# Hashing the later two pairs of a batch with GpSimd products and VectorE sums

## The chip, the cores and the metric

The kernel runs on one core of a Trainium2 chip. The metric is the device time of one execution in microseconds. The core has five engines that work side by side, each through its own queue in program order: TensorE (PE, with its weight loads as PEld), VectorE (DVE), ScalarE (ACT), GpSimd (POOL) and SyncE (SP), which here only issues DMAs. An engine whose next instruction waits does nothing else meanwhile.

## The reference, cut to what matters

Attention over 4 batches, 8 heads, 768 tokens and 64 dimensions, in which a query sees only the keys of its own hash bucket, followed by a gated feed-forward network with a residual:

```python
q_bits = (np.einsum('bhsd,dk->bhsk', q, proj) > 0).astype(np.int64)   # proj: 64 x 6
k_bits = (np.einsum('bhsd,dk->bhsk', k, proj) > 0).astype(np.int64)
...
mask = q_bucket[:, :, :, None] == k_bucket[:, :, None, :]
scores = np.where(mask, scale * q @ k.T, -1e9)
attn = exp(scores - max) / (sum + 1e-9);  x = attn @ v
g = x @ w_gate; val = x @ w_val
ffn_out = (gelu(g) * val) @ w_out
out = x + sigmoid(x @ w_res) * ffn_out
```

The hash gives six sign bits to each token and head: each is the sign of a product of a token's 64 numbers with a column of proj. It is computed in fp32.

## The kernel before, in words

Heads are handled in pairs, four pairs (p) to a batch, sixteen in all. "Side" 0 is q and side 1 is k. For one (pair, side) a tile `ld` of 128 partitions x 12 chunks x 64 holds the two heads' tokens. It is prepared in this way:

- `cast` (POOL, L184 for q and L186 for k) writes it as bf16 into the first 64 columns of a chunk of a `nat` tile. There are four `nat` tiles for all pairs, so that the later two pairs of a batch write where the earlier two were.
- `tr` (VectorE, L194) transposes 32 x 32 blocks of it into a `t32` tile, so that the 64 dimensions of 32 tokens stand on partitions, in two halves.
- `hash_mm` (TensorE, L205) multiplies `t32` with `projw`, a copy of proj in four blocks. One product of four (pair, side) jobs sits side by side; a call of `hashed` makes 16 of them, 32 matmul records.
- `hash_tok` (VectorE, L215) transposes the sums back, and `bits` (L224), four small instructions, one for each 32 partitions, writes +0.5 or -0.5 behind the 64 columns in `nat`.
- `turn` (L248) transposes `nat` into `aug` by a DMA that SP issues. `aug` is the operand of the score products, in which the bits make up the mask.

Each of the four batches goes through two stages. In the *scores stage* there are 36 slots, nine for a pair. A slot has the score products (`scores`, L380), an exponential on ScalarE (L385), some products of the previous batch's output projection (`project`: L431, L445, with VectorE's L448 and L451 after each of six token tiles), and the products with v of two slots ago (`values`, L354). After a head's values VectorE divides (`finish`, L306 and L307). A head's output buffer begins with a memset on VectorE (`opened`, L321), a product on TensorE (`preset`, L329) two slots later, and a copy on VectorE (`repeat`, L333), which the head's first values wait for. In slots counted from a stage's start, the memsets stand at 3, 7, 12, 16, 21, the copies at 5, 9, 14, 18, 23, and the first three L448 at 6, 13 to 14 and 21. Pair 2's scores begin at slot 18 and pair 3's at slot 27. ScalarE is busy for some 92% of this stage.

In the *gate stage* (`gate_val`) there are twelve steps m: eight products with w_gate and as many with w_val (L399), a Gelu on ScalarE (L416) and a product `hh` on VectorE (L419), which frees the buffer that the next step's w_val products need.

The order of everything else is written out by hand in two tables. `at(s, ...)` puts pieces behind the values of slot s, and `gv(b, m, ...)` puts them behind `hh` of step m of batch b's gate stage. For batch b + 1 the tables call its first two pairs `xs` and its later two `ys`. The x side is transposed and cast in the last slots of batch b's scores stage, hashed at the stage's end and in step 0, and gets its bits and turns in steps 0, 1, 2 and 4. The y side is transposed in slots 32 and 34 and in steps 3 and 5, cast in steps 5 and 6, hashed in step 6 (`hashed`), and gets its bits and turns in steps 7 to 10. The sums and the casts of v (`vals_s`: L281 to L285, `vals_a`: L273 and L274, all POOL) stand at slot 9p - 8. Weights are loaded by DMAs that POOL issues (L169); the last six stand in batch 0's gate stage, in steps 0, 0, 4, 5, 6 and 7. The first batch's own hash is done in another way and with TensorE, and does not change.

## Time and profile before

| | us |
|---|---|
| three runs | 346.91, 347.18, 347.49 (median 347.18) |
| span of the profiled execution | 344.9 |
| TensorE busy | 334.2 (97%) |
| ScalarE busy | 206.7 (60%) |
| VectorE busy | 191.4 (56%) |
| GpSimd busy | 86.3 (25%) |
| batch 0: scores stage, gate stage | to 47, 47 to 82.4 |
| batch 1: scores stage, gate stage | 82.4 to 125, 125 to 162.4 |
| batch 2: scores stage, gate stage | 162.4 to 205, 205 to 242.1 |
| batch 3: scores stage, gate stage and output | 242.1 to 285, 285 to 344.9 |

The page lists the profiled execution by its span alone, from its first to its last instruction; the times of the runs also hold what lies around it. In a line of the time line the first number is the start and the second the time from the start of the first to the end of the last instruction of the group; in square brackets stands how long the engine was idle before it, and whom it waited for. In a line of the groups stand the total, the mean of one in ns, and the idle time ahead with its releasers.

### The profile page before, as it was taken

The numbers are of one execution on the slowest core, as the hardware profiler recorded it, in microseconds if no ns is written. First come the engines' busy times: TensorE is split into PE (matmuls) and PEld (weight loads), VectorE is DVE, ScalarE is ACT, GpSimd is POOL, SyncE is SP. The second block draws the span as 40 slices with busy tenths as digits, with TensorE's granted clock in tenths as the row PEclk, the third lists the DMA queues.
The fourth block names the chain that finished last, engine by engine and source line by source line (L and its number), as shares of the span: only waits on it lengthen the run. The fifth ranks groups of instructions, "written<-read, shape, count | busy, mean of one in ns | idle before, by whom it ended". The sixth has DMA issues, their size and how long they took to land.

```text
span 344.9 us, 7549 instructions
## 1 busy us (share of the span) xinstructions
PE 334.2 (97%) x3064; PEld 204.3 (59%) x3112; DVE 191.4 (56%) x403; ACT 206.7 (60%) x232; POOL 86.3 (25%) x162
## 2 busy tenths in 40 slices
PE   7999999999999999999999999999999999999994
PEld 5667665655666655655666665655566665656442
DVE  7877757755345856757344784747244444333333
ACT  3789973226999962224999982323999984223110
POOL 4779940371055000270044100242030000000000
PEclk9999999999999999999999999999999999999999
DMA  7979999999375833528366642626330220000022
GB/s 224 376 62 219 205 276 217 197 139 193 103 188 172 204 106 78 102 38 149 82 193 188 231 115 65 128 48 113 72 100 32 55 55 30 32 1 0 32 77 76
DMA packets 71171, 42.90 MB, mean 124 GB/s; under 512 B 49504, under 2 KB 68192, under 8 KB 71136
## 3 DMA queue, kind: packets, MB, share of 16 engines
q1 hardware_dynamic: 64720, 37.17, 42.9%
q0 software_dynamic: 6336, 5.24, 10.8%
q8 instruction: 24, 0.39, 0.4%
q14 instruction: 11, 0.09, 0.1%
q10 hardware_dynamic: 80, 0.00, 0.0%
HBM read 29.36 MB, written 6.29 MB: 103 GB/s over the span
## 4 chain that ended last, share of the span: by engine, by line
PE 88%; ACT 4%; DVE 2%; DMA 2%; issue 2%; SPq 1%; POOL 0%; DVEq 0%; ACTq 0%
PE sp L399 36%; PE fps L445 18%; PE sp L380 15%; PE av L354 8%; PE rps L431 6%; ACT e L385 4%; PE hs L205 3%; DMA ld<-in_k_dram 2%; PE pt L259 1%; DVE o L451 1%; DVE nat L224 0%; SPq L96 0%; DVE o L448 0%; DVE ht L215 0%; DVE hh L419 0%
## 5 line engine op out<-in xcount | busy, mean ns | idle before, releaser
L385 ACT ACTIVATE e<-sp 128x1024 bf16<-128x1024 f32 x144 | 143.6, 1027 | 13.5 <-PE sp L380 8.0
L416 ACT ACTIVATE gt<-sp 128x768 bf16<-128x768 f32 x48 | 38.9, 811 | 92.5 <-PE sp L399 92.5
L380 PE MATMUL sp<-aug,aug 71*128 71x256 bf16 (+1 forms) x384 | 86.1, 325 | 1.1 <-ACT e L385 0.6
L445 PE MATMUL fps<-wo,hh 128*128 128x512 bf16 (+2 forms) x274 | 74.7, 369 | 1.6
L419 DVE TENSOR_TENSOR hh<-gt,sp 128x768 bf16<-128x768 bf16 x48 | 45.8, 954 | 50.1 <-PE sp L399 46.1
L399 PE MATMUL sp<-x_sb,wv 128*128 128x512 bf16 (+1 forms) x379 | 70.6, 325 | 0.4 <-DVE hh L419 0.2
L399 PE MATMUL sp<-x_sb,wg 128*128 128x256 bf16 (+1 forms) x373 | 70.4, 324 | 0.7
L354 PEld LDWEIGHTS <-e 128*128 128x128 bf16 x1152 | 53.3, 97 | 28.9 <-issue 1.2
L354 PE MATMUL av<-va,e 128*128 128x65 bf16 x1152 | 58.7, 193 | 0.1
L399 PEld LDWEIGHTS <-wv 128*128 128x128 bf16 x384 | 37.6, 98 | 25.1 <-issue 0.3
L399 PEld LDWEIGHTS <-wg 128*128 128x128 bf16 x384 | 36.8, 98 | 26.2 <-issue 2.3
L445 PEld LDWEIGHTS <-hh 128*128 128x128 bf16 x300 | 27.4, 97 | 22.7 <-issue 0.2
L448 DVE SCALAR_TENSOR_TENSOR o<-th,fps 128x512 f32<-128x512 f32 (+2 forms) x25 | 16.6, 666 | 36.6 <-PE fps L445 31.0
L380 PEld LDWEIGHTS <-aug 71*128 71x128 bf16 x384 | 29.4, 97 | 10.9 <-issue 2.2
L184 POOL TENSOR_SCALAR nat<-ld 128x768 bf16<-128x768 f32 (+1 forms) x16 | 13.8, 861 | 78.0 <-DMA aug<-nat 74.6
L281 POOL TENSOR_TENSOR v<-ldv 128x384 f32<-128x384 f32 x16 | 16.0, 999 | 67.7 <-DMA ldv<-in_v_dram 67.6
L194 DVE STREAM_TRANSPOSE t<-ld 128x768 f32<-128x768 f32 (+1 forms) x34 | 31.0, 916 | 1.4 <-DMA ld<-in_q_dram 0.7
L333 DVE COPY av<-av 128x390 f32<-128x390 f32 x24 | 13.6, 567 | 29.8 <-PE av L329 29.8
L431 PE MATMUL rps<-wr,x_sb 128*128 128x512 bf16 x90 | 25.3, 378 | 0.2
L435 ACT ACTIVATE th<-rps 128x512 f32<-128x512 f32 x24 | 14.2, 594 | 18.4 <-PE rps L431 18.4
L224 DVE TENSOR_SCALAR nat<-htp 32x72 bf16<-32x72 f32 x96 | 21.9, 229 | 1.8
L307 DVE TENSOR_TENSOR x_tok<-av,rec 128x384 bf16<-128x384 f32 x32 | 17.8, 557 | 1.1
(61 smaller groups left out, 190.7 us busy)
## 6 DMA issues: line engine op xcount, KB each, us to landing
ldv<-in_v_dram SPq DMA_DIRECT2D x16, 384.0 KB, 5.4
out_dram<-o SPq DMA_DIRECT2D x23, 256.0 KB, 2.0
ld<-in_q_dram SPq DMA_DIRECT2D x15, 384.0 KB, 5.4
ld<-in_k_dram SPq DMA_DIRECT2D x15, 384.0 KB, 6.2
wg<-in_moe_w_gate_dram POOLq DMA_DIRECT2D x4, 384.0 KB, 10.2
wv<-in_moe_w_val_dram POOLq DMA_DIRECT2D x4, 384.0 KB, 12.2
wo<-in_moe_w_out_dram POOLq DMA_DIRECT2D x3, 512.0 KB, 6.9
wr<-in_moe_w_res_dram POOLq DMA_DIRECT2D x1, 512.0 KB, 14.9
```

The source lines that it names most:

```text
L194: nc.vector.transpose(t32[p, side][:, sl].rearrange("p c h n -> p (c h n)"), raw[p, side][:, sl].rearrange("p c d -> p (c d)"))
L224: engs[a % len(engs)].tensor_scalar(nat_of(x)[32 * a:32 * a + 32, :, D:D + NBITS], ht[32 * j:32 * j + 32, :, NBITS * a:NBITS * (a + 1)], 0 ...
L307: nc.vector.tensor_mul(x_tok[b][:, hp, :, hi * D:(hi + 1) * D], o[:, 0:T, 0:D], rec.unsqueeze(2).to_broadcast([P, T, D]))
L354: nc.tensor.matmul(av[p, hi][:, qt, :], e[:, off:off + P], va[:, hi, jt, 0:D + 1], start=first, stop=(p >= HP and jt == T - 1), skip_group ...
L380: nc.tensor.matmul(sp[:, off:off + nq * P], ks[0:KA, hi * T + jt, :], qs[0:KA, hi * T + qt0:hi * T + qt0 + nq, :], start=True, stop=True)
L385: nc.scalar.activation(e, sp, AF.Exp, scale=float(ALPHA))
L399: nc.tensor.matmul(sp[:, c0:c1], w[:, kk, bass.ts(m, P)], xs[:, kk, c0:c1], start=(kk == 0), stop=(kk == KM - 1))
L416: nc.scalar.activation(gt, sp[:, 0:S], AF.Gelu)
L419: nc.vector.tensor_mul(hidden[b][:, m, :], gt, ps[1][:, 0:S])
L431: nc.tensor.matmul(rps, x_sb[b][:, kk, t, :], wr[:, kk, :], start=(kk == 0), stop=(kk == KM - 1))
L445: nc.tensor.matmul(fps[:, cs], hh[:, m, bass.ts(t, P)], wo[:, m, cs], start=(m == 0), stop=(m == KF - 1))
L448: nc.vector.scalar_tensor_tensor(o[:, cs], th[:, cs], 1.0, fps[:, cs], op0=ALU.add, op1=ALU.mult)
```

## The change

Only the y sides of batches 1 to 3 change. TensorE no longer hashes them. Instead, for each of the six columns j of proj, POOL multiplies the two halves of `t32` with a column of scalars (`pcol`, one number for each partition, made at the start by four copies ahead of those of `projw`), and VectorE sums the 32 rows of each block with a `tensor_reduce` that transposes the blocks as it reads them. In the *folded* form POOL also adds the two halves, and VectorE reads 384 elements per partition; in the *unfolded* form VectorE reads 768 and leaves two sums. After six columns `bits_sum` adds the two sums and writes the bits of all 128 partitions with one instruction, and the turn follows.

There are 24 parts for a batch, numbered n = 0 to 23: y 0 has parts 0 to 5, y 1 has 6 to 11, y 2 has 12 to 17, y 3 has 18 to 23. They are laid on 26 spots: spots 0 to 11 are the steps of the gate stage, spots 12 to 25 the slots in `BESIDE_SCORES` of the next scores stage. Part n stands at spot n and its sum at spot n + 2. Parts 0 to 9 are folded, 10 to 23 unfolded. So sums 0 to 9 stand in steps 2 to 11; sum 10 in slot 1; 11, 12 and 13 in slot 4; 14 and 15 in slot 7; 16 in 9; 17 in 11; 18 and 19 in 14; 20 to 23 in 16 to 19. The parts themselves take turns in two `pd` buffers. The transposes of y stand in steps 0, 4 and 10 and in slot 7, the turns of y in step 7 and in slots 4, 11 and 19.

The x side's bits and turns move to steps 1, 2, 3 and 5, the casts of y to steps 3, 4, 8 and 9, `vals_s` to slot 9p - 7 and `vals_a` to slot 9p - 5. The ring of `t32` tiles shrinks from six to four.

```diff
-    t32_pool = ctx.enter_context(tc.tile_pool(name="t32", bufs=6))
+    t32_pool = ctx.enter_context(tc.tile_pool(name="t32", bufs=4))
+    pd_pool = ctx.enter_context(tc.tile_pool(name="pd", bufs=2))
...
+    def part(x, j, fold):
+        if x not in hsums:
+            hsums[x] = sm_pool.tile([P, NBITS, HT, 2], FP32, tag="hsum", name="hsum")
+            nc.gpsimd.memset(hsums[x][:, :, :, 1], 0.0)
+        pd = pd_pool.tile([P, HT, 2, 32], FP32, tag="pd", name="pd")
+        for h in range(2):
+            nc.gpsimd.tensor_scalar(pd[:, :, h, :], t32[x][:, :, h, :], pcol[:, h, j:j + 1], None,
+                                    op0=ALU.mult)
+        if fold:
+            nc.gpsimd.tensor_add(pd[:, :, 0, :], pd[:, :, 0, :], pd[:, :, 1, :])
+        hparts[x, j] = pd
+
+    def part_sum(x, j, fold):
+        pd, s = hparts.pop((x, j)), hsums[x]
+        if fold:
+            nc.vector.tensor_reduce(s[:, j, :, 0], pd[:, :, 0, :], axis=mybir.AxisListType.X,
+                                    op=ALU.add, apply_transpose=True)
+        else:
+            nc.vector.tensor_reduce(s[:, j].rearrange("p c h -> p (c h)"),
+                                    pd.rearrange("p c h n -> p (c h) n"), axis=mybir.AxisListType.X,
+                                    op=ALU.add, apply_transpose=True)
+
+    def bits_sum(x):
+        s = hsums.pop(x)
+        nc.vector.tensor_add(s[:, :, :, 0], s[:, :, :, 0], s[:, :, :, 1])
+        nc.vector.tensor_scalar(nat_of(x)[:, :, D:D + NBITS],
+                                s[:, :, :, 0].rearrange("p j c -> p c j"), 0.0, 0.5,
+                                op0=ALU.is_gt, op1=ALU.subtract)
...
+    pcol = const.tile([P, 2, NBITS], FP32, name="pcol")
+    spread(lambda a: pcol[32 * a:32 * a + 32], [nc.gpsimd] * 4)
     spread(lambda a: projw[32 * a:32 * a + 32, :, NBITS * a:NBITS * (a + 1)], [nc.gpsimd] * 4)
...
+    BESIDE_SCORES = (1, 4, 4, 4, 7, 7, 9, 11, 14, 14, 16, 17, 18, 19)
...
-            if j < 2:
-                at(s0 + 32 + 2 * j, lambda y=y: tr(*y))
...
-        for m, x in zip((0, 1, 2, 4), xs):
+        for m, x in zip((1, 2, 3, 5), xs):
             lay(b, m, x)
-        gv(b, 3, lambda y=ys[2]: tr(*y))
-        gv(b, 5, lambda y=ys[3]: tr(*y))
-        for m, y in zip((5, 5, 6, 6), ys):
+        for m, y in zip((3, 4, 8, 9), ys):
             gv(b, m, lambda y=y: cast(*y, nc.gpsimd))
-        gv(b, 6, lambda p0=p0: hashed((p0 + 2, p0 + 3)))
-        gv(b, 7, lambda p0=p0: tokens((p0 + 2, p0 + 3), True))
-        for m, y in zip((7, 8, 9, 10), ys):
-            lay(b, m, y)
+        s1 = s0 + NSLOT
+        spots = [(gv, (b, m)) for m in range(KF)]
+        spots += [(at, (s1 + t,)) for t in BESIDE_SCORES]
+        work = [(y, j) for y in ys for j in range(NBITS)]
...
+        for n, (y, j) in enumerate(work):
+            fold = n + 2 < KF
+            if j == 0:
+                put(max(0, n - 2), lambda y=y: tr(*y))
+            put(n, lambda y=y, j=j, fold=fold: part(y, j, fold))
+            put(n + 2, lambda y=y, j=j, fold=fold: part_sum(y, j, fold))
+            if j == NBITS - 1:
+                put(n + 2, lambda y=y: bits_sum(y), lambda y=y: turn(*y))
     for p in range(HP, NPAIR):
-        at(9 * p - 8, lambda p=p: vals_s(p), lambda p=p: vals_a(p))
+        at(9 * p - 7, lambda p=p: vals_s(p))
+        at(9 * p - 5, lambda p=p: vals_a(p))
         loads(9 * p - 20, (p, "v"))
```

More of the change, by code (lines that the diff above doesn't have):

```diff
@@ L243, in bits_one @@
                                 hs[:, 1, :, 0:NBITS], 0.0, 0.5, op0=ALU.is_gt, op1=ALU.subtract)
+    hsums, hparts = {}, {}
+    def part(x, j, fold):
[24 more added lines that the diff above has]
+                                op0=ALU.is_gt, op1=ALU.subtract)
     def turn(p, side):
@@ L585, with put @@
         gv(b, 0, lambda p0=p0: tokens((p0, p0 + 1), True))
-        for m, x in zip((0, 1, 2, 4), xs):
+        for m, x in zip((1, 2, 3, 5), xs):
             lay(b, m, x)
-        gv(b, 3, lambda y=ys[2]: tr(*y))
-        gv(b, 5, lambda y=ys[3]: tr(*y))
-        for m, y in zip((5, 5, 6, 6), ys):
+        for m, y in zip((3, 4, 8, 9), ys):
             gv(b, m, lambda y=y: cast(*y, nc.gpsimd))
-        gv(b, 6, lambda p0=p0: hashed((p0 + 2, p0 + 3)))
-        gv(b, 7, lambda p0=p0: tokens((p0 + 2, p0 + 3), True))
-        for m, y in zip((7, 8, 9, 10), ys):
-            lay(b, m, y)
+        s1 = s0 + NSLOT
+        spots = [(gv, (b, m)) for m in range(KF)]
+        spots += [(at, (s1 + t,)) for t in BESIDE_SCORES]
+        work = [(y, j) for y in ys for j in range(NBITS)]
+        def put(n, *pieces):
+            where, x = spots[n]
+            where(*x, *pieces)
+        for n, (y, j) in enumerate(work):
[6 more added lines that the diff above has]
+                put(n + 2, lambda y=y: bits_sum(y), lambda y=y: turn(*y))
     for p in range(HP, NPAIR):
-        at(9 * p - 8, lambda p=p: vals_s(p), lambda p=p: vals_a(p))
+        at(9 * p - 7, lambda p=p: vals_s(p))
+        at(9 * p - 5, lambda p=p: vals_a(p))
         loads(9 * p - 20, (p, "v"))
```

## The prediction

> **What bounds the kernel now.** I read the page's busy table and its chain first, then the time line of one gate stage, then the stage table of one scores stage.
>
> ```profile
> span 344.9 us, 7549 instructions
> PE 334.2 (97%) x3064; PEld 204.3 (59%) x3112; DVE 191.4 (56%) x403; ACT 206.7 (60%) x232; POOL 86.3 (25%) x162
> PE sp L399 36%; PE fps L445 18%; PE sp L380 15%; PE av L354 8%; PE rps L431 6%; ACT e L385 4%; PE hs L205 3%; DMA ld<-in_k_dram 2%; PE pt L259 1%; DVE o L451 1%; DVE nat L224 0%; SPq L96 0%; DVE o L448 0%; DVE ht L215 0%; DVE hh L419 0%
> ```
>
> TensorE carries the chain, and hash products (L205) are 3% of it. POOL and VectorE look free, but these are averages. In a gate stage, twelve steps m each end with one product hh (L419) on VectorE:
>
> ```profile
> 65.52 0.95 DVE L419 TENSOR_TENSOR hh<-gt,sp 128x768 bf16<-128x768 bf16 x1 [0.63 <-PE sp L399]
> 67.94 1.51 PE L205 MATMUL hs<-t,projw 128*32 128x192 f32 x32
> 68.12 0.95 DVE L419 TENSOR_TENSOR hh<-gt,sp 128x768 bf16<-128x768 bf16 x1 [0.76 <-PE sp L399]
> 72.26 0.95 DVE L419 TENSOR_TENSOR hh<-gt,sp 128x768 bf16<-128x768 bf16 x1 [3.19 <-PE sp L399]
> 73.14 0.59 DVE L215 STREAM_TRANSPOSE htp<-hs 128x384 f32<-128x384 f32 x1
> 73.76 0.93 DVE L224 TENSOR_SCALAR nat<-htp 32x72 bf16<-32x72 f32 x4
> 74.86 0.95 DVE L419 TENSOR_TENSOR hh<-gt,sp 128x768 bf16<-128x768 bf16 x1 [0.17 <-PE sp L399]
> ```
>
> A step lasts 68.12 - 65.52 = 2.60 us. The one with the later pairs' 32 hash records lasts 4.14. The last row is a step in which VectorE had 2.47 us of work and still waited 0.17 us for TensorE: 2.5 us per step is what VectorE can hold.
>
> **Gain: the hash leaves TensorE.** 4.14 - 2.60 = 1.54 us, in three batches (the chain in order of time has the other two):
>
> ```profile
> 148.00 1.44 PE hs L205 x32
> ...
> 227.76 1.44 PE hs L205 x32
> ```
>
> -4.6 us. Two transposes of hash sums and 32 bit writes also leave VectorE's gate stage; they were hidden.
>
> **Loss at the start: four copies into pcol.**
>
> ```profile
> 9.96 0.82 POOL L186 CAST nat<-ld 128x768 bf16<-128x768 f32 x1 [0.52 <-DMA ld<-in_k_dram]
> 10.73 0.88 POOL L144 COPY projw<-projn 32x12 f32<-32x12 f32 x4
> 11.66 0.47 PEld L205 LDWEIGHTS hs<-t,projw 128*32 128x32 f32 x8 [0.65 <-POOL projw L144]
> ```
>
> The copies stand between the cast and projw on POOL's queue, have the same shape as the four of L144, and TensorE already waits for projw there. They cost what those cost, 0.88 us, and the exponentials behind it have idle time for TensorE, so nothing takes it up: +0.9.
>
> **Prices of the new operations.**
>
> ```profile
> L194 DVE STREAM_TRANSPOSE t<-ld 128x768 f32<-128x768 f32 x30 | 28.8, 963 | 0.7 <-DMA ld<-in_k_dram 0.6
> L194 DVE STREAM_TRANSPOSE t<-ld 128x384 f32<-128x384 f32 x4 | 2.2, 565 | 0.7 <-DMA ld<-in_q_dram 0.7
> L306 DVE RECIPROCAL rec<-av 128x6 f32<-128x6 f32 x32 | 6.1, 192 | 16.1 <-PE av L354 13.4 <-PE av L326 2.4
> L242 DVE TENSOR_SCALAR nat<-hs 128x36 bf16<-128x36 f32 x4 | 0.8, 195 | 0.1
> L281 POOL TENSOR_TENSOR v<-ldv 128x384 f32<-128x384 f32 x16 | 16.0, 999 | 67.7 <-DMA ldv<-in_v_dram 67.6
> L283 POOL TENSOR_TENSOR v<-v 128x128 f32<-128x128 f32 x16 | 7.3, 458 | 1.3
> L284 POOL TENSOR_TENSOR vsum<-v,v 128x128 bf16<-128x128 f32 x16 | 7.4, 460 | 1.3
> L184 POOL TENSOR_SCALAR nat<-ld 128x768 bf16<-128x768 f32 x15 | 13.3, 884 | 77.2 <-DMA aug<-nat 74.6 <-issue 2.0 <-DMA ld<-in_q_dram 0.5
> L184 POOL TENSOR_SCALAR nat<-ld 128x384 bf16<-128x384 f32 x1 | 0.5, 517 | 0.7 <-DMA ld<-in_q_dram 0.7
> L224 POOL TENSOR_SCALAR nat<-ht 32x72 bf16<-32x72 f32 x6 | 2.9, 481 | 3.7 <-DVE ht L215 3.3
> L169 POOL DMA_DIRECT2D wo<-in_moe_w_out_dram x3 | 2.4, 792 | 0.0
> ```
>
> A sum over transposed blocks reads what a transpose reads and writes less. I take the transpose's time: 0.57 us for a folded part (384), 0.96 us for an unfolded one (768). Lower end 0.88, because independent VectorE instructions start up to 0.08 us before the one ahead ends (72.26 to 73.14 is 0.88 for a duration of 0.95); upper end 1.9, a transpose and a second pass. A product of 384 elements is 0.52 us by L184. Its lower end is 0.46, the same overlap on POOL (9.96 to 10.73 for 0.82). For the upper end take L224: 0.48 us for 72 elements is mostly fixed cost, and 312 more at L184's slope of (884 - 517)/384 = 0.96 ns give 0.78. I stay at 0.52, the nearest in shape. The fold is L281's shape, 1.00. So a folded part is 2.03 us of POOL, an unfolded one 1.03. The two instructions that make bits of the sums are 0.2 each by L306 and L242.
>
> On the column operand: the Trainium skill, GPSIMD Engine Reference, § 7, says that each small read command costs about 102 cycles which do not overlap with the one before. If a column of scalars were such a command, a product would take an estimated 0.60 us and the sum below would be the second rival's 357. L224 leans that way, L184 does not decide it.
>
> **Gate stage.** VectorE in m 2, 3 and 5: hh 0.95, bits 0.95, a sum 0.57, together 2.47. In m 4 and 10 a transpose stands for the bits, 2.48. Both fit, as the step at 72.26 did; without that 0.1 us, TensorE would pay what exceeds 2.6. POOL in ten steps: 10 x 2.03 + 4 casts x 0.82 = 23.6 of 26.0 us. The casts of y wait for the DMA turns of x in the same buffers, with parts queued behind them:
>
> ```profile
> 133.12 0.93 DVE L224 TENSOR_SCALAR nat<-htp 32x72 bf16<-32x72 f32 x4
> ...
> 137.96 0.83 POOL L184 TENSOR_SCALAR nat<-ld 128x768 bf16<-128x768 f32 x1 [27.87 <-DMA aug<-nat]
> ```
>
> From the end of the bits to the cast is 3.9 us; the change leaves two steps, 5.2. The turn costs nothing then, and if it came later the sums two steps on would cover some 2 us.
>
> **Scores stage, where it is decided.** Fourteen unfolded sums, one transpose and three pairs of bit instructions move into slots 0 to 21. Slot 0 begins at 162.4 in this batch:
>
> ```profile
> 162.40:189.33 26.93, 26.65 (x285) 16.45 (x288) 11.04 (x24) 25.18 (x27) 7.84 (x13) 1.00 0.56 154
> ```
>
> The columns are length, PE, PEld, DVE, ACT, POOL. VectorE has 11.04 us now. Added: 14 x 0.96 + 0.96 + 6 x 0.2 = 15.6. That is 26.7 of 26.9 us, and the gaps between small instructions now have to be filled without a wait. Two things prevent it.
>
> ```profile
> 162.65 0.95 DVE L419 TENSOR_TENSOR hh<-gt,sp 128x768 bf16<-128x768 bf16 x1 [0.63 <-PE sp L399]
> 168.77 0.57 DVE L333 COPY av<-av 128x390 f32<-128x390 f32 x1 [5.04 <-PE av L329]
> 170.11 0.41 PE L354 MATMUL av<-va,e 128*128 128x65 bf16 x8
> 179.13 0.96 DVE L451 SCALAR_TENSOR_TENSOR o<-o,x_tok 128x512 f32<-128x512 f32 x1
> 179.55 1.22 POOL L184 TENSOR_SCALAR nat<-ld 128x768 bf16<-128x768 f32 x1
> 188.79 0.11 DVE L321 MEMSET av<- 128x65 f32 x1
> 189.33 0.19 PE L329 MATMUL av<-vsum,eps_sb 128*128 128x65 bf16 x1
> ```
>
> First, slot 4's last sum (number 13) waits for POOL. Part 11 reuses the buffer that sum 9 frees after hh of m 11, at 162.65 + 0.95 + 0.57 = 164.2. Then part 11 (165.2), part 12 (166.3), the v sums of the next pair, put at slot 2 (0.999 + 0.458 + 0.460 + 0.1 = 2.0, 168.3), part 13 (169.3). Sum 13 ends at 170.3 and the copy L333 behind it at 170.9. Its readers are the second half of the values at 170.11, some 170.2: TensorE stands 0.7 us. VectorE, done with sum 12 at about 167.5, has lost 1.8 us.
>
> Second, L451 took 0.96 us beside a POOL instruction and 0.69 without; with POOL nearly always busy two more will. +0.3.
>
> So VectorE reaches the memset of slot 21 at 162.65 + 26.7 + 1.8 + 0.3 = 191.4, and TensorE wants it at 189.3: 2.1 us late (the 0.7 is within it). Overlap at some ten instructions gives back 0.5 and rounding the rest; I take 1.8 a batch, three batches, +5.4. After slot 21 no sums remain and VectorE catches up.
>
> The Trainium skill, SBUF — State Buffer, § Who interferes with whom, says that a VectorE instruction with two SBUF inputs contends with GpSimd's reads, and that a reduction never does. The two rows at 179 agree with the first half; by the second the sums keep their price, which no run here shows.
>
> **Batch 0 has more on POOL**: four weight loads queued at m 4 to 7, 4 x 0.79 = 3.2 us, which today run early. 23.6 + 3.2 + about 1 us of waiting for buffers = 27.8 of 26.0: part 9 ends some 1.8 us behind, and through parts 10 to 13 about 1.3 us of it reaches the same sum 13. +1.3. The last of the four is issued in m 7 or 8, at least three steps (7.8 us) ahead of the scores stage, and lands in 6.9:
>
> ```profile
> wo<-in_moe_w_out_dram POOLq DMA_DIRECT2D x3, 512.0 KB, 6.9
> ```
>
> Moved at no cost: the v casts and sums (at slots 2 and 4 instead of 1) are read five slots on; the turns of y on SP's queue stand at slots 4, 11 and 19, and slot 19 + 3.9 us is before slot 27's first use; SP's loads behind them are for the next batch. The smaller t32 ring is freed by the hash of x before m 0's transpose.
>
> **Sum.** -4.6 + 0.9 + 5.4 + 1.3 = +3.0. The page lists the profiled execution by its span, 344.9; the median, 347.18, is 2.3 above it and I leave that difference unchanged: span 347.9, time 350.2.
>
> **Rivals.**
> First, faster: the sums follow each other at 0.88 and the products at 0.46. VectorE's load is 25.4, and sum 13's chain ends 0.6 earlier; each batch loses about 0.4, batch 0 another 0.4. -4.6 + 0.9 + 1.2 + 0.4 = -2.1, 345.1. It decides when VectorE is through slot 21's memset by 189.3. For it: the overlap rows. Against: a sum that waits for POOL cannot start early. With no stall at all it is 343.5.
> Second, POOL becomes the bound: a product with a scalar column takes 0.60. Ten folded parts are 1.7 us longer, parts 10 to 13 another 0.7: sum 13 comes 2.4 later in each batch, +7.2: 357. For it: L224's fixed cost. Against: L184 at the same size.
> Third, the transposed sum is slower than the transpose, say by 0.3: 14 x 0.3 x 3 = 12.6, and some in the gate stage: 363. Nothing in the trace speaks for a second pass, nothing excludes it.
>
> **Numbers.** Forecast 0.37 (its own range 348.3 to 353), first rival 0.28, second 0.20, third 0.10, stalls that just cancel the gain 0.05. The range, 344.5 to 358, leaves out a gain without stalls and the third rival. Within 0.2% (0.7 us, about what a measurement tells from no change): 0.05. Faster 0.28, slower 0.67.
>
> **What would show it.** Right: no L205 group with 32 records in m 6, hh steps at 2.60 throughout; L205's first wait 0.9 longer; sums of 0.57 and 0.96; an idle stretch on VectorE ahead of sum 13 released by POOL, and TensorE waiting for L333 at slot 5 and for the memset at slot 21. Wrong: products far from 0.52, sums far from 0.96, or TensorE without waits in slots 4 to 21.

## The result, and the profile after

The changed kernel takes 436.03 us (median of four runs, 434.90 to 437.44) against 347.05 us for the kernel before on the same chip: a ratio of 1.257, with an interval of 1.254 to 1.260. The forecast was 350.2 and the range ended at 358. The direction was right, the size was not: 89 us are lost instead of 3.

The page of the changed kernel shows it at once: the span, the busy time of the engines, the slices of TensorE, GpSimd and the granted clock, and the chain by engine and by line.

```profile
span 434.8 us, 7602 instructions
...
PE 354.9 (82%) x2969; PEld 210.6 (48%) x3016; DVE 241.1 (55%) x448; ACT 208.3 (48%) x232; POOL 293.9 (68%) x352
...
PE   8999997664795999877488599997728759999995
...
POOL 4879389999999506999999940699999980000000
PEclk9999999898696999999869789999997988999999
...
POOL 52%; PE 33%; DVE 6%; ACT 3%; issue 3%; DMA 2%; SPq 1%; POOLq 0%; DVEq 0%; ACTq 0%
POOL pd L254 38%; PE fps L477 9%; PE sp L431 9%; POOL pd L257 7%; PE sp L412 6%; PE av L386 4%; ACT e L417 3%; PE rps L463 3%; DMA ld<-in_k_dram 2%; POOL nat L187 1%; DVE hsum L266 1%; POOL nat L185 1%; POOL va L305 1%; PE hs L206 1%; DVE o L480 1%
```

Before, TensorE had nearly the whole chain. Now GpSimd has 52% of it, and the products of `part` (L254) alone 38%. GpSimd is at 9 in three long stretches, and in most slices of these TensorE is at 8 or less, once at 2. They are the gate stages with the first 20 slots or so of the scores stage behind them, where the parts lie.

The groups of the same kernel, with shapes kept apart (total, mean of one in ns, idle time ahead and its releaser):

```profile
L254 POOL TENSOR_SCALAR pd<-t,pcol 128x384 f32<-128x384 f32 x144 | 177.9, 1251 | 48.1 <-DVE t L195 48.0
L266 DVE TRANSPOSE_TENSOR_REDUCE hsum<-pd 128x24 f32<-128x768 f32 x42 | 40.9, 973 | 48.4 <-POOL pd L254 48.3
L263 DVE TRANSPOSE_TENSOR_REDUCE hsum<-pd 128x12 f32<-128x384 f32 x30 | 17.4, 578 | 50.2 <-POOL pd L257 50.0
L257 POOL TENSOR_TENSOR pd<-pd 128x384 f32<-128x384 f32 x30 | 29.8, 994 | 2.5
L185 POOL TENSOR_SCALAR nat<-ld 128x768 bf16<-128x768 f32 x15 | 13.3, 886 | 1.3 <-DMA ld<-in_q_dram 1.2
```

The sums and the fold cost what was forecast: 0.973, 0.578 and 0.994 us against 0.96, 0.57 and 1.00. The product costs 1.251 us, not 0.52, and lies far outside the ends of 0.46 and 0.78. The row to set beside it is L185, the cast (L184 before), from which the price was taken: it handles twice the elements in 0.886 us.

With this price a folded part is 2 x 1.25 + 0.99 = 3.5 us of GpSimd instead of 2.03. Ten of them and four casts are 38.5 us, in a gate stage that had 31.0. The gate stages of batches 1 and 2, from the first L451 (`hh`) to the last, now last 38.04 and 38.03 us (before 31.02 and 31.02). That this is so near the 38.5 is partly chance: the first part waits 2.4 us for its transposed tile, and the last `hh` stands behind sum 8, so that nine parts and three casts lie ahead of it, some 34 us, in which GpSimd makes no pause. Batch 0, with four weight loads on the same queue, takes 41.49 (before 30.43). From the last `hh` of a stage to the first of the next one it is 69.03, 70.53 and 70.27 us, where it was 48.97, 48.74 and 48.38. Together with 1.4 us more before the first `hh` (53.64 against 52.23) and 0.3 less in the last part, that is the whole difference of the two spans: 25.1 + 63.7 + 1.4 - 0.3 = 89.9.

The stage table of the changed kernel for the first scores stage, in two stretches (length, then PE, PEld, DVE, ACT and POOL busy, granted clock, DMA share, GB/s), and under it two rows of TensorE's time line from the second stretch:

```profile
99.00:141.00 42.00, 27.47 (x255) 15.93 (x259) 25.22 (x43) 21.83 (x24) 41.53 (x47) 0.80 0.40 98
108.00:116.00 8.00, 4.28 (x27) 2.40 (x28) 5.20 (x9) 2.22 (x3) 8.00 (x9) 0.51 0.28 85
```

```profile
111.50 0.38 PE L386 MATMUL av<-va,e 128*128 128x65 bf16 x4 [7.99 <-DVE av L365]
112.95 1.06 PE L463 MATMUL rps<-wr,x_sb 128*128 128x512 bf16 x2 [0.22 <-issue]
```

GpSimd is busy for 41.5 of 42.0 us, and VectorE, which was to be full here, for 25.2. The releaser in brackets is the forecast's own place, the copy of slot 5 (L365), behind sum 13 on VectorE's queue. TensorE waits there for 7.99 us instead of 0.7. In the second stretch, which holds the end of that wait and the 4.5 us behind it, its granted clock is 0.51. The Trainium skill, TensorE: Matmul & The Clock Gate, Part 1, says that TensorE falls to half its clock after an idle window of about 3.4 us; the 0.51 behind 7.99 us agrees with that. How much of the 89 us is slower clock and how much waiting was not separated, since GpSimd was the bound at that time in any case.

### The profile page after: what moved, and what is told of

The parts are those of the page before. It is cut to its first block, busy times and chain, and to the rows that moved or that the text cites. A ratio compares the mean times of both kernels' runs of the same rounds, so it can differ in the third digit from the quotient of the medians.

```text
span 434.8 us, 7602 instructions
## 1 busy us (share of the span) xinstructions
PE 354.9 (82%) x2969; PEld 210.6 (48%) x3016; DVE 241.1 (55%) x448; ACT 208.3 (48%) x232; POOL 293.9 (68%) x352
## 4 chain that ended last, share of the span: by engine, by line
POOL 52%; PE 33%; DVE 6%; ACT 3%; issue 3%; DMA 2%; SPq 1%; POOLq 0%; DVEq 0%; ACTq 0%
POOL pd L254 38%; PE fps L477 9%; PE sp L431 9%; POOL pd L257 7%; PE sp L412 6%; PE av L386 4%; ACT e L417 3%; PE rps L463 3%; DMA ld<-in_k_dram 2%; POOL nat L187 1%; DVE hsum L266 1%; POOL nat L185 1%; POOL va L305 1%; PE hs L206 1%; DVE o L480 1%
## 5 line engine op out<-in xcount | busy, mean ns | idle before, releaser
L254 POOL TENSOR_SCALAR pd<-t,pcol 128x384 f32<-128x384 f32 x144 | 177.9, 1251 | 48.1 <-DVE t L195 48.0
L412 PE MATMUL sp<-aug,aug 71*128 71x256 bf16 (+1 forms) x384 | 93.0, 346 | 7.7 <-DVE hh L451 6.7
L386 PE MATMUL av<-va,e 128*128 128x65 bf16 x1152 | 63.1, 199 | 36.6 <-DVE av L365 36.2
L386 PEld LDWEIGHTS <-e 128*128 128x128 bf16 x1152 | 57.2, 101 | 70.9 <-issue 33.4
L431 PE MATMUL sp<-x_sb,wg 128*128 128x512 bf16 (+1 forms) x374 | 71.4, 328 | 0.6
L266 DVE TRANSPOSE_TENSOR_REDUCE hsum<-pd 128x24 f32<-128x768 f32 x42 | 40.9, 973 | 48.4 <-POOL pd L254 48.3
L451 DVE TENSOR_TENSOR hh<-gt,sp 128x768 bf16<-128x768 bf16 x48 | 45.2, 942 | 26.7 <-PE sp L431 22.3
L263 DVE TRANSPOSE_TENSOR_REDUCE hsum<-pd 128x12 f32<-128x384 f32 x30 | 17.4, 578 | 50.2 <-POOL pd L257 50.0
L257 POOL TENSOR_TENSOR pd<-pd 128x384 f32<-128x384 f32 x30 | 29.8, 994 | 2.5
L463 PE MATMUL rps<-wr,x_sb 128*128 128x512 bf16 x91 | 29.3, 423 | 0.5 <-issue 0.4
L483 DVE SCALAR_TENSOR_TENSOR o<-o,x_tok 128x512 f32<-128x512 f32 (+2 forms) x25 | 18.4, 736 | 0.9
```

Of the source, the lines that this page charges most:

```text
L254: nc.gpsimd.tensor_scalar(pd[:, :, h, :], t32[x][:, :, h, :], pcol[:, h, j:j + 1], None, op0=ALU.mult)
L257: nc.gpsimd.tensor_add(pd[:, :, 0, :], pd[:, :, 0, :], pd[:, :, 1, :])
L266: nc.vector.tensor_reduce(s[:, j].rearrange("p c h -> p (c h)"), pd.rearrange("p c h n -> p (c h) n"), axis=mybir.AxisListType.X, op=ALU.a ...
L386: nc.tensor.matmul(av[p, hi][:, qt, :], e[:, off:off + P], va[:, hi, jt, 0:D + 1], start=first, stop=(p >= HP and jt == T - 1), skip_group ...
L412: nc.tensor.matmul(sp[:, off:off + nq * P], ks[0:KA, hi * T + jt, :], qs[0:KA, hi * T + qt0:hi * T + qt0 + nq, :], start=True, stop=True)
L431: nc.tensor.matmul(sp[:, c0:c1], w[:, kk, bass.ts(m, P)], xs[:, kk, c0:c1], start=(kk == 0), stop=(kk == KM - 1))
```

## The experiments

**What makes a product cost 1.25 us?** Several properties were new against the cast from which the price came: a column as the scalar, gaps in the views, the split into 384, an fp32 output, and a single operation where the cast, as written in the kernel, has two. A first group of runs took the first three away, one at a time.

With a constant in place of the column (the output is then not the reference's):

```diff
-            nc.gpsimd.tensor_scalar(pd[:, :, h, :], t32[x][:, :, h, :], pcol[:, h, j:j + 1], None,
+            nc.gpsimd.tensor_scalar(pd[:, :, h, :], t32[x][:, :, h, :], 0.5, None,
                                     op0=ALU.mult)
```

> The products multiply by the constant 0.5 instead of the column of scalars (so the later two pairs of batches 1 to 3 get bits of no meaning); all shapes, queues and waits stay. Theory A (the operand that is a column of scalars makes a product 1.25 us): products fall to about 0.52 us and the time to what the prediction made of that price, 348 to 353. Theory B (the rows of 32 with gaps between them do it) and theory C (VectorE's traffic beside it does it): products stay at 1.25 us and the time near 436.

The group of its products:

```profile
L254 POOL TENSOR_SCALAR pd<-t 128x384 f32<-128x384 f32 x144 | 166.6, 1178 | 48.2 <-DVE t L195 48.1
```

422.43 us, a ratio of 1.218 [1.213, 1.222]. The column costs about 0.07 us of each product. That is the effect for which the prediction quoted the Trainium skill, GPSIMD Engine Reference, § 7 (0.08 us more on a product by the prediction's estimate from the page); the run agrees with the size. Whether the column is such a read command no run shows. It is not what makes the product slow.

The same elements, each half of the tile read and written without gaps (the pairing of elements and columns is then another):

```diff
-            nc.gpsimd.tensor_scalar(pd[:, :, h, :], t32[x][:, :, h, :], pcol[:, h, j:j + 1], None,
-                                    op0=ALU.mult)
+            nc.gpsimd.tensor_scalar(pd[:, h * T:h * T + T], t32[x][:, h * T:h * T + T],
+                                    pcol[:, h, j:j + 1], None, op0=ALU.mult)
```

> The column of scalars stays, but a product reads and writes 384 elements without gaps (chunks 0 to 5 or 6 to 11, both halves, so the sums have no meaning). Theory A: 1.25 us and about 436 as before. Theory B: about 0.52 us and 348 to 353. Theory C: 1.25 us.

```profile
L254 POOL TENSOR_SCALAR pd<-t,pcol 128x384 f32<-128x384 f32 x144 | 177.5, 1247 | 48.3 <-DVE t L195 48.2
```

434.83 us, 1.254 [1.251, 1.257]: the gaps cost nothing.

One product over all 768 elements with one column, which leaves out the second half's own scalars:

```diff
-        for h in range(2):
-            nc.gpsimd.tensor_scalar(pd[:, :, h, :], t32[x][:, :, h, :], pcol[:, h, j:j + 1], None,
-                                    op0=ALU.mult)
+        nc.gpsimd.tensor_scalar(pd, t32[x], pcol[:, 0, j:j + 1], None, op0=ALU.mult)
```

> One product over all 768 elements with one column instead of two over 384 (the upper half is multiplied by the wrong numbers). If the extra 0.73 us is a fixed cost of each instruction that takes a column, one lasts about 1.25 + 0.37 = 1.6 us, and a folded part falls from 3.5 to 2.6 us: the time falls by 25 us or more. If it is a cost for each element, one lasts 2.3 to 2.5 us and the time stays within some us of 436.

```profile
L253 POOL TENSOR_SCALAR pd<-t,pcol 128x768 f32<-128x768 f32 x72 | 159.7, 2225 | 46.6 <-DVE t L195 46.5
```

414.83 us, 1.196 [1.194, 1.199]. By the means, (2225 - 1251) / 384 = 2.5 ns for each further element, where the cast's slope was 0.96. So it is no fixed cost of an instruction; each element is slow. The time fell by 21 us, more than expected for this case; 72 instructions fewer, at the 0.28 us that is left of 1.251 without 384 x 2.5 ns, are 20 us on GpSimd.

**And without the products?** The products and the fold are left out, and the sums read `t32` itself; the output is then not the reference's.

```diff
-        pd = pd_pool.tile([P, HT, 2, 32], FP32, tag="pd", name="pd")
-        for h in range(2):
-            ...
-        if fold:
-            nc.gpsimd.tensor_add(pd[:, :, 0, :], pd[:, :, 0, :], pd[:, :, 1, :])
-        hparts[x, j] = pd
+        hparts[x, j] = t32[x]
```

> GpSimd's products and folds are left out and the sums read the transposed tile itself (bits of no meaning); VectorE's work, the order of all else and the copies into pcol stay. By the prediction's steps without any wait for GpSimd: -4.6 + 0.9, and VectorE late by 0.3 to 0.6 us in each of three scores stages, so -2 to -3 us: 344 to 345.5. Rival (VectorE's added load alone stalls TensorE by more than the hash had cost): 348 or more.

346.23 us, 0.998 [0.996, 0.999], between the 344 to 345.5 that the prediction's steps gave and its rival's 348. So the loss of 89 us is in the products and folds, and their waits. Two rows of TensorE's time line, the first scores stage:

```profile
101.16 0.28 PE L380 MATMUL av<-va,e 128*128 128x65 bf16 x4 [0.37 <-DVE av L359]
110.69 0.19 PE L355 MATMUL av<-vsum,eps_sb 128*128 128x65 bf16 x1 [0.78 <-DVE av L347]
```

With GpSimd's parts out of the way VectorE's added work alone costs 1.5, 1.1 and 0.5 us in the three scores stages (50.43, 49.85 and 48.85 us), at the forecast's places: the memset of slot 21 in all three (0.78, 0.95 and 0.30 us), the copy of slot 5 in the first. The gate stages' ordinary steps are 2.60 us. The gain is given back in good part here already. The two instructions that make the bits take 0.36 and 0.31 us in this run:

```profile
L267 DVE TENSOR_SCALAR nat<-hsum 128x72 bf16<-128x72 f32 x12 | 4.3, 360 | 0.4
L266 DVE TENSOR_TENSOR hsum<-hsum 128x72 f32<-128x72 f32 x12 | 3.7, 310 | 0.6
```

**The other terms of the sum.** What the removed hash was worth: the kernel before, with the y sides' hash left out and the bits of the x sides used again (not the reference's output).

```diff
-        ht, j = htok.pop(x)
+        p0 = p - p % HP
+        ht, j = htok[p if p < HP or p < p0 + 2 else p - 2, side]
...
-        gv(b, 6, lambda p0=p0: hashed((p0 + 2, p0 + 3)))
-        gv(b, 7, lambda p0=p0: tokens((p0 + 2, p0 + 3), True))
```

> The kernel before with the hash of the later two pairs of batches 1 to 3 left out (their bits are taken from the earlier two pairs' sums), nothing put in its place. The prediction's first term: -4.6 us, 342.4. Rival (another wait fills the gap): less than -2.

342.27 us against 346.76, 0.987 [0.986, 0.988]: -4.5, forecast -4.6.

What the four copies cost: the kernel before, with `pcol` made but not used.

```diff
+    pcol = const.tile([P, 2, NBITS], FP32, name="pcol")
+    spread(lambda a: pcol[32 * a:32 * a + 32], [nc.gpsimd] * 4)
     spread(lambda a: projw[32 * a:32 * a + 32, :, NBITS * a:NBITS * (a + 1)], [nc.gpsimd] * 4)
```

> The kernel before with the four copies into pcol and nothing else of the change. The prediction's second term: +0.9 us, 347.9. Rival (the start has slack for them): 0.0 to +0.2.

347.35 us, 1.0018 [1.0009, 1.0027]: +0.6 (+0.3 to +0.9), forecast +0.9. The profiled execution doesn't show the forecast's path: its hash product starts at 12.19 without a wait, behind score products that already come 0.75 us later than before. In the ten profiled kernels with the copies ahead of `projw`, the product's wait for `projw` is anything from 0 to 1.15 us (0.70 in the change).

And the other way round: the kernel before, with the copies of `projw` moved ahead of the first `vals_a`.

```diff
+    spread(lambda a: projw[32 * a:32 * a + 32, :, NBITS * a:NBITS * (a + 1)], [nc.gpsimd] * 4)
     vals_a(0)
     ...
-    spread(lambda a: projw[32 * a:32 * a + 32, :, NBITS * a:NBITS * (a + 1)], [nc.gpsimd] * 4)
```

> The kernel before with the four copies into projw moved ahead of the first v cast on GpSimd's queue, where GpSimd stood idle 1.1 us for a DMA. If the start has no slack for these copies, as the second term says, TensorE's 0.65 us wait for projw goes: -0.4 to -0.7 us. If the start has slack: no difference.

346.65 us, 0.9996 [0.9987, 1.0005]: no difference. TensorE's time line around its first hash product (L205), in the kernel before and in this one:

```profile
10.91 0.60 PE L380 MATMUL sp<-aug,aug 71*128 71x512 bf16 x2
11.66 0.84 PE L205 MATMUL hs<-t,projw 128*32 128x192 f32 x8 [0.15 <-POOL projw L144]
```

```profile
11.16 0.60 PE L380 MATMUL sp<-aug,aug 71*128 71x512 bf16 x2
11.69 0.84 PE L205 MATMUL hs<-t,projw 128*32 128x192 f32 x8
```

Before, the product waits 0.15 us for `projw`; the 0.65 us of the prediction's row is the wait of the weight load, most of which passes while the score products ahead are still running. Here the wait is gone. There were 0.15 us to gain, less than these runs tell apart; in this execution the score products also begin 0.25 us later. So the forecast's reading, that TensorE already waits for `projw`, rests on 0.15 us.

**A product of another kind.** The column stretched over the elements and multiplied as a second tensor; same output.

```diff
-            nc.gpsimd.tensor_scalar(pd[:, :, h, :], t32[x][:, :, h, :], pcol[:, h, j:j + 1], None,
-                                    op0=ALU.mult)
+            nc.gpsimd.tensor_mul(pd[:, :, h, :], t32[x][:, :, h, :],
+                                 pcol[:, h, j:j + 1].unsqueeze(1).to_broadcast([P, HT, 32]))
```

> The products as products of two tensors, the second a column read again for every element, in place of the scalar operand; results as in the changed kernel. By the tensor addition of the same size a product lasts 1.0 us, so a folded part 3.0 instead of 3.5 us and an unfolded one 2.0 instead of 2.5: the chain's GpSimd share falls by about a sixth, 400 to 425. If the repeated read costs more: 436 or above.

```profile
L254 POOL TENSOR_TENSOR pd<-t,pcol 128x384 f32<-128x384 f32 x144 | 116.7, 837 | 53.1 <-DVE t L195 46.4 <-DVE hsum L266 4.2 <-DVE hsum L263 2.4
```

379.86 us, 1.095 [1.093, 1.097], where 1.0 us a product and 400 to 425 were expected. A product with two inputs is cheaper than the one with a scalar, 0.84 us against 1.25. So the single-operation form itself was suspect, and two theories were left for it: its output type (the cast writes bf16), or its one operation. Two runs tell them apart. First a second operation that changes no value:

```diff
-            nc.gpsimd.tensor_scalar(pd[:, :, h, :], t32[x][:, :, h, :], pcol[:, h, j:j + 1], None,
-                                    op0=ALU.mult)
+            nc.gpsimd.tensor_scalar(pd[:, :, h, :], t32[x][:, :, h, :], pcol[:, h, j:j + 1], 1.0,
+                                    op0=ALU.mult, op1=ALU.mult)
```

> The changed kernel with a second operation in the product, a multiplication by 1.0, as the casts of q have it; results as in the changed kernel. After the immediate and the gapless views left the product at 1.17 to 1.25 us, what still sets it apart from the cast of 0.52 us is that it has one operation where the cast has two (theory D) and that it writes fp32 where the cast writes bf16 (theory E). D: products at 0.52 to 0.6 us, and the time at what the prediction made of these prices, 350 to 357. E: products at 1.25 us or more and the time at 436.

and then one operation with a bf16 output (the sums read `t32`, so the output is not the reference's):

```diff
-        pd = pd_pool.tile([P, HT, 2, 32], FP32, tag="pd", name="pd")
+        pd = pd_pool.tile([P, HT, 2, 32], BF16, tag="pd", name="pd")
...
-        hparts[x, j] = pd
+        hparts[x, j] = t32[x]
```

> The products with one operation but written as bf16, into tiles that nothing but the fold reads; the sums read the transposed tile, as where the products were left out (bits of no meaning), so VectorE does not wait for GpSimd. D: products stay at 1.25 us. E: 0.52 to 0.6 us. The time is not what this run is for: GpSimd still delays the casts and v sums if products are slow.

The product's group with two operations, with the rows of the two instructions that make the bits:

```profile
L254 POOL TENSOR_SCALAR pd<-t,pcol 128x384 f32<-128x384 f32 x144 | 82.5, 588 | 60.8 <-DVE t L195 48.0 <-DVE hsum L263 6.1 <-DVE hsum L266 4.4
L273 DVE TENSOR_SCALAR nat<-hsum 128x72 bf16<-128x72 f32 x12 | 8.5, 711 | 0.4
L272 DVE TENSOR_TENSOR hsum<-hsum 128x72 f32<-128x72 f32 x12 | 5.2, 435 | 0.4
```

and with one operation and bf16 output:

```profile
L254 POOL TENSOR_SCALAR pd<-t,pcol 128x384 bf16<-128x384 f32 x144 | 178.2, 1252 | 35.0 <-DVE t L195 34.9
```

That settles it: 0.588 us with a multiplication by 1.0 more, 1.252 with another output type and one operation. With two operations the kernel takes 355.04 us, 1.025 [1.023, 1.027]; the 81 us between it and the change are the price of leaving the second operation out. This kernel is also nearly the change as the prediction had priced it (0.59 against 0.52 us), so the places of its stalls can be read there. TensorE's time line, batch 0's gate stage and the first scores stage:

```profile
75.72 1.46 PE L431 MATMUL sp<-x_sb,wv 128*128 128x512 bf16 x8 [0.44 <-DVE hh L451]
84.74 0.59 PE L412 MATMUL sp<-aug,aug 71*128 71x256 bf16 x3 [0.85 <-DVE hh L451]
89.78 0.38 PE L477 MATMUL fps<-wo,hh 128*128 128x512 bf16 x1 [1.13 <-DMA wo<-in_moe_w_out_dram]
93.54 0.28 PE L386 MATMUL av<-va,e 128*128 128x65 bf16 x4 [1.02 <-DVE av L365]
114.66 0.19 PE L361 MATMUL av<-vsum,eps_sb 128*128 128x65 bf16 x1 [1.44 <-DVE av L353]
```

and VectorE's, with sum 13 and the L483 of a token tile:

```profile
92.05 0.98 DVE L266 TRANSPOSE_TENSOR_REDUCE hsum<-pd 128x24 f32<-128x768 f32 x1 [1.28 <-POOL pd L254]
102.69 1.25 DVE L483 SCALAR_TENSOR_TENSOR o<-o,x_tok 128x512 f32<-128x512 f32 x1
```

The scores stages are 52.94, 51.79 and 51.43 us, +4.0, +3.1 and +3.1 over before; the gate stages 30.77, 29.77 and 29.77 (28.88, 29.48 and 29.48 with the hash left out). The row at 89.78 is in batch 0 alone: the last load of w_out, which GpSimd issues at 76.28, lands 13.5 us later.

**Can it gain at all?** From here on all products have two operations. ScalarE makes four of the 24 parts, as it has idle time in the gate stage (`AF.Copy` with `pcol` as its scale). Fourteen sums stand in the gate stage and the other ten are spread over slots 1 to 18; `pcol` is made after the first v sums, the weight loads of batch 0 all stand in step 0, and `pd` has a third buffer.

```diff
-    for m in (0, 0, 4, 5, 6, 7):
+    for m in (0, 0, 0, 0, 0, 0):
...
+            if a:
+                nc.scalar.activation(pd[:, :, h, :], t32[x][:, :, h, :], AF.Copy,
+                                     scale=pcol[:, h, j:j + 1])
...
-    BESIDE_SCORES = (1, 4, 4, 4, 7, 7, 9, 11, 14, 14, 16, 17, 18, 19)
+    GATE_SUMS = {0: 2, 1: 3, 2: 4, 3: 5, 4: 6, 5: 6, 6: 7, 7: 8, 8: 8, 9: 9, 10: 9, 11: 10, 12: 11, 13: 11}
+    LATE = {14: (10, 13), 15: (11, 14), 16: (13, 16), 17: (14, 16), 18: (16, 19), 19: (16, 21), ...}
+    ACT_PARTS = {8, 10, 5, 13}
```

> The products with two operations, and work moved to where engines are free: ScalarE, idle for 1.8 us of each gate step, makes the products of parts 5, 8, 10 and 13 (unfolded), so that 14 of the 24 sums stand in the gate stage and 10 in slots 1 to 18 of the scores stage; pcol is made after the start's v sums, batch 0's six weight loads all stand in step 0, and pd has three buffers. If the rest of the loss is what the prediction's scores-stage step says (VectorE full in slots 0 to 21, sum 13 behind GpSimd) and batch 0's loads, then with 3.8 us less of VectorE there and no loads in GpSimd's way the stalls fall below 1 us a batch: 343.5 to 346.5, at or below the kernel before. Rival (gate steps now overflow on VectorE or the Gelu comes late behind ScalarE's products): 348 to 354.

354.69 us, 1.023 [1.021, 1.024], just past the rival's 348 to 354 and far from the expected 343.5 to 346.5. The scores stages are within 0.3 us of before (49.02, 49.01, 48.64), but the gate stages lose. Its time line, GpSimd and TensorE:

```profile
68.27 0.83 POOL L186 TENSOR_SCALAR nat<-ld 128x768 bf16<-128x768 f32 x1 [7.03 <-DMA aug<-nat]
72.94 2.72 PE L437 MATMUL sp<-x_sb,wv 128*128 128x512 bf16 x8 [3.60 <-DVE hh L457]
83.08 1.46 PE L437 MATMUL sp<-x_sb,wg 128*128 128x512 bf16 x8 [0.85 <-ACT gt L454]
```

In batch 0 a cast waits 7.03 us for a turn, with the parts queued behind it, and TensorE then waits 3.60 us for `hh`. All six weight loads are under way at the same time: those of w_out land 15 to 20 us after their issue. (That the turn was late because of them is read from the order, not tried alone.) In the last row TensorE also waits 0.85 us for a Gelu on ScalarE, which now has products in its queue; batches 1 and 2 have the same wait.

The next version spreads the loads of batch 0 over steps 0, 0, 0, 4, 6 and 8, gives ScalarE three parts, and keeps thirteen sums in the gate stage:

```diff
-    for m in (0, 0, 0, 0, 0, 0):
+    for m in (0, 0, 0, 4, 6, 8):
...
+    GATE_SUMS = {0: 2, 1: 3, 2: 4, 3: 5, 4: 6, 5: 6, 6: 7, 7: 8, 8: 8, 9: 9, 10: 10, 11: 10, 12: 11}
+    LATE = {13: (10, 13), 14: (11, 14), 15: (13, 16), 16: (14, 16), 17: (16, 17), 18: (19, 21), ...}
+    BITS_AT = {5: 7, 11: 11, 17: 19, 23: 30}
+    ACT_PARTS = {8, 11, 5}
```

> The run before freed the scores stage (its three lengths are within 0.3 us of the kernel before's) but lost in the gate stage: 5.9 us in batch 0, where the casts of y stood 7 us behind a DMA turn that the early weight loads slow, and 1.4 us in each later batch, from step 1 with one transpose too many, step 7 with sums and bits together, and step 9, where a product on ScalarE waits for a pd buffer and the Gelu stands behind it. Here three parts only (5, 8, 11) go to ScalarE, at steps where their buffer is free, the third transpose moves to step 9, the bits to steps 7 and 11, and batch 0's last three loads to steps 4, 6 and 8. If these are the causes, gate stages come within 0.5 us of the shortest seen (28.9 in batch 0, 29.5 later) while the scores stages stay: -2 to -4.5 us against the kernel before, 342.5 to 345. Rival (the work only moves the stall, and 13 sums beside the scores are already too many): 347 or more.

347.26 us, 1.0022 [1.0007, 1.0036], again the rival's outcome (342.5 to 345 was expected). The gate stages are now 29.01, 29.47 and 29.47, within 0.13 us of those with the hash left out. What is lost stands in the scores stages (51.6, 50.02, 49.41). The table of slots 0 to 21, and one row each of VectorE, TensorE and GpSimd:

```profile
81.48:108.41 26.93, 24.68 (x258) 14.82 (x261) 22.42 (x40) 23.03 (x25) 22.70 (x44) 1.00 0.59 146
```

```profile
87.55 0.99 POOL L319 TENSOR_TENSOR v<-ldv 128x384 f32<-128x384 f32 x1
...
90.80 0.98 DVE L272 TRANSPOSE_TENSOR_REDUCE hsum<-pd 128x24 f32<-128x768 f32 x1 [1.74 <-POOL pd L260]
...
92.40 0.59 PE L483 MATMUL fps<-wo,hh 128*128 128x512 bf16 x2 [1.04 <-DVE o L486]
```

VectorE has 22.4 us of work in 26.9 and still makes TensorE wait. The sum at 90.80 waits 1.74 us for its products, and these stand on GpSimd behind the v sums that begin at 87.55. So the next version changes little but that order: the v sums go from slot 9p - 7 to 9p - 5, the v casts from 9p - 5 to 9p - 4; sum 17 goes from slot 5 to 7 and a transpose from slot 7 to 5.

```diff
-    LATE = {..., 17: (16, 17), ...}
+    LATE = {..., 17: (16, 19), ...}
-    TRS = (0, 4, 9, 19)
+    TRS = (0, 4, 9, 17)
...
-        at(9 * p - 7, lambda p=p: vals_s(p))
-        at(9 * p - 5, lambda p=p: vals_a(p))
+        at(9 * p - 5, lambda p=p: vals_s(p))
+        at(9 * p - 4, lambda p=p: vals_a(p))
```

> From the run before: its gate stages are within 0.1 us of those with the hash left out, and what it loses stands in the scores stages, 51.6, 50.0 and 49.4 us against 49.0, 48.7 and 48.4. There sum 17 waited 1.74 us for GpSimd, whose part 17 stood behind 2 us of v sums, and L448, the memset and TensorE came late one after another. Here the v sums move two slots and the v casts one slot later, behind the products of slot 4, sum 17 to slot 7 and the last transpose to slot 5. If GpSimd's order is the cause, the scores stages come within 0.5 us of the kernel before's and the time to 343 to 345.5. If VectorE's load is (11 unfolded sums beside the scores), they stay above by 1 us or more each and the time at 346 to 348.

The page's busy row and the table of slots 0 to 21:

```profile
PE 329.4 (97%) x2969; PEld 201.7 (59%) x3016; DVE 239.4 (70%) x448; ACT 216.2 (64%) x250; POOL 189.3 (56%) x334
```

```profile
81.00:107.90 26.90, 26.62 (x285) 16.41 (x288) 24.37 (x43) 25.14 (x27) 25.32 (x46) 1.00 0.61 156
```

342.12 us, 0.987 [0.985, 0.988]: this version is 1.3% faster than the kernel before, a little better than the expected 343 to 345.5, and it is level with the one that leaves the hash out (342.27). With 24.4 us on VectorE and 25.3 on GpSimd in 26.9, TensorE is busy for 26.62. Nothing is left of the 3 to 4 us a batch.

**The order alone, in the change itself.** The mixed versions also took work off VectorE. The last run keeps the change with two operations, all 14 late sums included, and moves only the v sums and casts as above.

> The change with two operations in its products, and the v sums moved from slot 9p - 7 to 9p - 5 and the v casts from 9p - 5 to 9p - 4, so that on GpSimd they stand behind parts 13 to 15 instead of ahead of part 13. All 14 late sums stay on VectorE. If GpSimd's order is what stalls the scores stages (order theory): sum 13's wait falls from 1.28 to 0.3 us or less, TensorE's waits of 1.02 (copy) and 1.44 (memset of slot 21) shrink to what the sums cost without products, 0.37 and 0.78 or less, and the time falls from 355.0 to 350 to 353. If VectorE's load is what stalls them (load theory, the prediction's): the waits move by no more than a few tenths and the time stays at 354 to 356. Batch 0's gate stage is the same in both, some 2 us over the others.

351.83 us, 1.015 [1.013, 1.017]. TensorE's waits for this work in the first scores stage are now these:

```profile
91.86 0.28 PE L386 MATMUL av<-va,e 128*128 128x65 bf16 x4 [0.16 <-DVE av L365]
95.40 0.19 PE L361 MATMUL av<-vsum,eps_sb 128*128 128x65 bf16 x1 [0.39 <-POOL vsum L317]
113.03 0.19 PE L361 MATMUL av<-vsum,eps_sb 128*128 128x65 bf16 x1 [1.12 <-DVE av L353]
```

Sum 13 no longer waits; the copy of slot 5 costs 0.16 us instead of 1.02, the v sums are themselves late by 0.39 now, and the memset of slot 21 is late by 1.12, more than the 0.78 that was expected at most. The scores stages are 51.17, 50.88 and 50.51. So both theories hold a share: the order was worth 3.2 us of the whole time (in batch 0 with part of the wait for the w_out load, which falls from 1.13 to 0.15 us), and about 2.1 us a batch are left. In slots 0 to 21 VectorE is busy for 25.70 of 27.40 us there, and the rest is nearly all three waits for GpSimd's products (0.69, 0.54 and 0.45 us):

```profile
85.50:112.90 27.40, 25.61 (x278) 15.52 (x277) 25.70 (x45) 24.15 (x26) 25.52 (x49) 1.00 0.79 169
```

## Why the prediction was right or wrong

**The step that failed is the price of the product**: "A product of 384 elements is 0.52 us by L184 ... I stay at 0.52, the nearest in shape." It was nearest in shape, but L184 does two operations to each element and the product does one, and on GpSimd that form takes 1.25 us, against 0.59 with a second operation. The upper end, 0.78 from L224, has the same flaw: it too has two operations, and the other GpSimd rows from which prices were taken were copies or had two inputs. So the bounds bounded nothing. The Trainium skill, GPSIMD Engine Reference, § 4.1, says that GpSimd runs elementwise work on one input at roughly line rate and is slower with two; here the order was reversed for the form with one operation (1.25 us with one input, 0.84 and 0.99 with two), and the measurement decides; with two operations (0.59) the order was the page's.

**What followed from it** was the second rival's mechanism, at a price that it did not have: POOL as the bound. It was given 0.60 us a product and a time of 357. At 0.59 the kernel takes 355.0; that this is near the rival's time is luck, since the rival had sum 13 come 2.4 us later than the forecast, and sum 13 waits 1.28 us where the forecast had 1.8. At 1.25, GpSimd is the bound and the time is 436.

**The right terms.** The gain was -4.5 (forecast -4.6). The two transposes and 32 writes that the prediction says leave VectorE are one and 16 a batch (3 and 48 in all); they were hidden either way. The sums were 0.578 and 0.973 (0.57 and 0.96; so the third rival, a second pass, is out), and 0.574 and 0.944 where GpSimd made no products. The fold was 0.99 (1.00). The start was +0.6 (+0.9): right within its interval, but not by the path forecast, since TensorE's products had waited only 0.15 us for `projw`. The gate stage's ordinary steps hold 2.60 us when products cost 0.59.

**The scores stage: right places, too small a sum.** At 0.59 the forecast's waits are all there: sum 13 for POOL (1.28 us; 1.8 forecast), the copy of slot 5 (1.02; 0.7), the memset of slot 21 (1.44; 2.1). But each is added, where the forecast had the 0.7 within the 2.1, and the stages lose 3.1 to 4.0 us instead of 1.8. Part of it is a mis-sized term: the two instructions that make the bits take 0.71 + 0.44 us, not 0.2 each, so with three such pairs in these slots VectorE's load is some 2 us a batch higher; and an L483 beside GpSimd took 1.25 us, not 0.96. With no parts on GpSimd the two cost 0.36 + 0.31, so over half of their excess comes with GpSimd's work; by what path wasn't tried.

**That VectorE's load decides was half right.** The first rival was to decide when VectorE is through by slot 21. With the v sums moved the loss falls from between 3.1 and 4.0 us a batch to 2.1 with VectorE's instructions unchanged, and in the fastest version VectorE does 24.4 of 26.9 us with no stall. About 0.9 us a batch was GpSimd's order, which the forecast had seen (its first reason); in batch 0 the fall is 1.8 us, with the late load in it. Of the 2.1 that are left, VectorE's own load explains 0.5 to 1.5, by the run without products; the forecast had it at nearly nothing once the wait was taken off. The rest comes with the parts on GpSimd and was not taken apart.

**Batch 0** cost 2.5 us more than the others at 0.59 (forecast +1.3): 1.6 of it already in its own gate stage, where steps 8 and 11 last 3.24 and 3.86 us, and 0.9 in the scores stage behind it. The forecast let all of it slip to the scores stage, through sum 13, and had the last weight load land 6.9 us after its issue, in time and at no cost. It took 13.5, and TensorE waited 1.13 us for it. In the last run, where that wait is 0.15 us, batch 0's scores stage loses no more than the others (2.2 against 2.1), which points to the late load as the cause of these 0.9 us.

## What to carry to other kernels

A row is a price for another instruction only if the operation is the same, not only the shape: engine, number of operations, number of inputs, and types; where the trace has no such row, the upper end must come from a far one, several times the nearest. On this GpSimd a scalar product with a harmless second operation (times 1.0) was 2.1 times as fast as without. And where an engine in order feeds another one, look at what stands ahead of the feeding piece before cutting the fed engine's load: moving the v sums two slots and the v casts one gained 3.2 us in one version and 5.1 in another (there with a sum and a transpose moved as well), with the same work.

## What the runs showed of the hardware

- GpSimd's `tensor_scalar` with one operation on fp32: 1.25 us for 384 elements in each partition and 2.22 for 768; 1.18 with a constant as the scalar; 1.25 with bf16 output and 1.25 without gaps. With two operations 0.59. A tensor times a stretched column 0.84, two full tensors 0.99. Why the single operation is slower isn't shown by any of them.
- VectorE's sum over transposed blocks costs what a plain transpose does: 0.578 us for 384 and 0.973 for 768 elements (transposes 0.565 and 0.963).
- ScalarE makes the same product in 0.607 us (the Gelu behind it on its queue then made TensorE wait 0.85 us):

```profile
L257 ACT ACTIVATE pd<-t,pcol 128x384 f32<-128x384 f32 x24 | 13.4, 607 | 14.7 <-DVE hsum L269 8.2 <-DVE hsum L272 6.4
```

- TensorE's granted clock was 0.51 in the 8 us around the end of a wait of 7.99 us, and 0.80 over the 42 us of that scores stage in which the parts lie, while in the version with two operations, where the longest wait read in that stage was 1.44 us, the mean clock over the execution was 0.998.
